# Agent attention and gated convolution: loads held to a fixed time ahead of use, and other rows in the shifted copies

## The chip, the cores and the metric

The kernel runs on one core of a Trainium2 chip. The core has TensorE (PE, matrix products into PSUM), VectorE (DVE), ScalarE (ACT), GpSimd (POOL) and SyncE (SP, which here issues nearly all DMAs). The time of a run is in microseconds on the device; several runs are made and the median is told. The profile is one further look at a single execution: its span goes from the first to the last instruction of the program.

## What is computed

Two stages. First agent attention: 49 agents gather from 12800 keys, and 12800 queries gather from the agents. Then a gated unit with a causal convolution of 5 taps.

```python
def sm(a, b):                       # softmax over the last axis
    s = scale * (a @ b.transpose(0, 2, 1))
    s = s - s.max(-1, keepdims=True)
    e = np.exp(s)
    return e / (e.sum(-1, keepdims=True) + 1e-09)
a2k = sm(agents, k)                 # (4, 49, 12800)
agent_v = a2k @ v                   # (4, 49, 128)
q2a = sm(q, agents)                 # (4, 12800, 49)
x = q2a @ agent_v                   # (4, 12800, 128)
...
for k in range(K):                  # K = 5, xp is x with 4 rows of zeros ahead
    gate_pre += conv_w[k][None, None, :] * xp[:, k:k + S, :]
gate = 1.0 / (1.0 + np.exp(-gate_pre))
val = x @ w_val
out = gate * val @ w_out
```

q, k, v have shape (4, 12800, 128), agents (4, 49, 128).

## The kernel before

The x of the reference is never formed. The attention weights q2a (49 numbers a row) are themselves the input of the gated stage, and agent_v is folded into the weights of that stage once a batch: `fold_weights` makes, for each of the 5 taps and for w_val, a matrix that takes 128 rows of attention weights to 128 channels.

**Units and chunks.** A batch of 12800 rows is cut into 10 units of 1280 rows for the attention and into 25 chunks of 512 rows for the gated stage. Two units, that is five chunks, make a segment of 2560 rows. There are 4 batches, 40 units, 20 segments and 100 chunks (the last one in two halves).

**Steps.** Each unit has a key step k (`key_scores`: 16 score matmuls at L376, a copy on ScalarE, a maximum on DVE), a value step v (`agent_values`: exponentials, a block transpose on DVE, 40 matmuls at L480), a query step q (`queries`) and a transpose step t (`transposes`). Each chunk has a gate step g (`gates`: five matmuls at L922, one at L926, a tanh at L935), a value step a (`values`: L949, L953, the product h at L962, its upper half hh at L968 on ScalarE, its lower half hl at L973 on GpSimd) and an output step o (`project`: L992 to L994, a scaled copy at L1006, the store). "max" and "fold" are the key maximum and the folding of weights, once a batch.

**Precision by pairs.** Products of the gated stage are made in fp16 from sums of an upper and a lower half. A weight of 49 agents is thus 49 numbers upper and 49 lower, and products upper x upper, lower x upper and upper x lower are wanted: 147 rows for a matrix that has 128. So `queries` builds the tile pt with 128 columns a row: 49 lower halves (L794, GpSimd), 49 upper halves (L779, ScalarE), and 30 of the upper halves a second time (L784, GpSimd), to be met with the lower halves of the folded weights. The 19 agents that don't fit go into a second stationary: for these, x2 holds 19 x 5 = 95 rows, each agent's upper half at the five shifts of the convolution, and L926 and L953 multiply them. Which agents are doubled in pt and which 19 go to x2 is a choice; the folded weights in `wst` (tile rows 2A and up, and the rows TAPS+1 and TAPS+2) must follow the same choice. Before, of the first 45 agents two in three are doubled in pt and every third goes to x2 with the last four.

**Transposes and shifts.** pt must be turned, so that its 128 columns lie on partitions. For the first four units PE does that; for the others a DMA transpose from pt into the tile x1 (L835). Then `shifts` copies the 19 rows of x1, five times each at shifts of one element, into x2 by two DMAs (L884), one for each entry of X2CUTS: 15 source partitions with step 3, then 4 with step 1. From the third segment on this is done once for a segment, behind the transpose of its second unit. `halo` copies the last 4 columns of a segment to the head of the next, on GpSimd (L819).

**Loads.** `load` brings a unit of k, q or v into one of NLOAD = 11 slots of the tile ld, in the order of use (L369). A load may start when the last use of its slot is done.

**The plan.** Nothing is issued at once. Each step is put into a `Plan` with its engine, a cost in us, and what it reads and writes. PE's steps keep their order, which is written out by hand in a long string. `Plan.order` then plays the steps through: it keeps a time for each engine, lets the engine that can start first do so, takes among the open steps the one with the longest tail of work behind it, and models the DMA by one wire with a cost for each transfer (1.57 for a load, 2.4 for a transpose, the numbers in X2CUTS for x2). A step is open from the time `at` that its inputs are ready. The steps are emitted sorted by their start in this play. Each engine's queue, SP's too, then runs in that order on the chip; the times of the play are not kept, only the order. A load has no input but its free slot, so in the play it is open as soon as the slot is.

Of the kernel before, what the change touches and what calls it, by code (L numbers as in the profile page):

```python
# [13 lines left out]
ALU = mybir.AluOpType  # L14
# [13 lines left out]
TAPS = 5  # L28
HALO = TAPS - 1
PAD = 16  # L30


THREES = 15
NDUP = 2 * THREES
X2R = 19
X2CUTS = ((0, THREES, 3, 0.5), (THREES, X2R, 1, 0.3))


NLOAD = 11
# [1 line left out]
NPT = 4  # L41
# [17 lines left out]
BACKLOG = 3.0  # L59
LANES = 8  # L60
LAND = 1.4

QS = 256.0
WS = 64.0
# [3 lines left out]
class Plan:  # L68
# [11 lines left out]
    def add(self, engine, us, fn, reads=(), writes=(), moved=0.0, key=None, urge=0.0):  # L80
        i = len(self.steps)
        need = set()
        for x in reads:
            need |= self.wrote.get(x, set())
        for x in writes:
            need |= self.wrote.get(x, set()) | self.read.get(x, set())
        for x in reads:
            self.read.setdefault(x, set()).add(i)
        for x in writes:
            self.wrote[x], self.read[x] = {i}, set()  # L90
        self.steps.append((engine, us, fn, need, moved, key))
        self.urge.append(urge)

    def order(self):
        n = len(self.steps)
        after = [[] for _ in range(n)]
        last = None
# [16 lines left out]
        wire = 0.0  # L114
        lanes = [0.0] * LANES
        left = [len(s[3]) for s in self.steps]
        at = [0.0] * n
        queues = {e: [] for e in engines}
        pe = [i for i, s in enumerate(self.steps) if s[0] == "pe"]
        here = 0  # L120
# [50 lines left out]
                        queues[self.steps[j][0]].append(j)  # L171
        self.start = start
        return sorted(range(n), key=lambda i: (start[i], i))


@with_exitstack
def tile_agent_attention_gated_conv(
# [9 lines left out]
    nc = tc.nc  # L187
# [166 lines left out]
    def load(kind, b, u):  # L354
        i = taken[0] % NLOAD
        taken[0] += 1
        slot_of[kind, b, u] = i
        if kind == "v":
            dst, src = ld[i], vP[b, u].rearrange("p n c -> p (n c)")
        else:  # L360
            dst = ld[i][:, 0:UNIT]
            src = (kT if kind == "k" else qT)[b, :, u * UNIT : (u + 1) * UNIT]
        parts = [(dst, src, [("ld", i), ("ld2", i)])]
        if (kind, b, u) == ("v", 0, NU - 1):
            h = VW // 2
            parts = [(dst[:, 0:h], src[:, 0:h], [("ld", i)]), (dst[:, h:], src[:, h:], [("ld2", i)])]
        for d, f, keys in parts:
            add(
                "dma", 0.4, lambda d=d, f=f: nc.sync.dma_start(out=d, in_=f), (), keys,  # L369
                1.57 / len(parts),  # L370
            )

    def score_matmuls(b, src, out):
# [139 lines left out]
    def fold_weights(b):  # L513
# [58 lines left out]
        ghi = wst[:, 0:TAPS, 0:A]  # L572
        vhi = wst[:, TAPS, 0:A]

        def threes(x):

            if len(x.shape) == 2:
                return x[:, 0 : 3 * THREES].rearrange("p (i r) -> p i r", r=3)
            return x[:, :, 0 : 3 * THREES].rearrange("p k (i r) -> p k i r", r=3)

        def rest(out, full, s, hi):
            dve.scalar_tensor_tensor(
                out=out, in0=full, scalar=rs[:, s : s + 1], in1=hi,
                op0=ALU.mult, op1=ALU.subtract,
            )

        def val_weights():
            dve.tensor_reduce(
                out=mx[:, 1:2], in_=pv[:, 0:A], axis=AX.X, op=ALU.max,
                apply_absolute_value=True,  # L590
            )
            dve.tensor_scalar(
                out=mx[:, 1:2], in0=mx[:, 1:2], scalar1=TINY, scalar2=1.0 / WS,
                op0=ALU.max, op1=ALU.mult,
            )
            dve.reciprocal(out=rs[:, 1:2], in_=mx[:, 1:2])
            dve.tensor_scalar_mul(vhi, pv[:, 0:A], rs[:, 1:2])
            pv3, hi3 = threes(pv[:, 0:A]), threes(vhi)
            rest(
                wst[:, TAPS, 2 * A :].rearrange("p (i r) -> p i r", r=2),  # L600
                pv3[:, :, 0:2], 1, hi3[:, :, 0:2],
            )
            rest(x2v[:, HALO, 0:THREES], pv3[:, :, 2], 1, hi3[:, :, 2])
            rest(x2v[:, HALO, THREES:], pv[:, 3 * THREES : A], 1, vhi[:, 3 * THREES :])

        def gate_weights():
            dve.tensor_scalar_mul(ghi, gw, rs[:, 0:1])
# [6 lines left out]
        def gate_rest_pool():  # L614
            def less(out, full, hi):
                nc.gpsimd.tensor_tensor(out=out, in0=full, in1=hi, op=ALU.subtract)

            gs3, hi3 = threes(gs), threes(ghi)
            twos = wst[:, 0:TAPS, 2 * A :].rearrange("p k (i r) -> p k i r", r=2)
            for r in range(2):  # L620
                less(twos[:, :, :, r], gs3[:, :, :, r], hi3[:, :, :, r])
            less(x2g[:, :, 0:THREES], gs3[:, :, :, 2], hi3[:, :, :, 2])
            less(x2g[:, :, THREES:], gs[:, :, 3 * THREES :], ghi[:, :, 3 * THREES :])

        def gate_rest():
            gw3, hi3 = threes(gw), threes(ghi)
            twos = wst[:, 0:TAPS, 2 * A :].rearrange("p k (i r) -> p k i r", r=2)
            for r in range(2):
                rest(twos[:, :, :, r], gw3[:, :, :, r], 0, hi3[:, :, :, r])
            rest(x2g[:, :, 0:THREES], gw3[:, :, :, 2], 0, hi3[:, :, :, 2])  # L630
            rest(x2g[:, :, THREES:], gw[:, :, 3 * THREES :], 0, ghi[:, :, 3 * THREES :])

        w_ = ("wst", x)

# [98 lines left out]
    def queries(b, u):  # L733
# [28 lines left out]
        def sums():  # L762
# [16 lines left out]
            "act", 0.58, lambda: nc.scalar.copy(out=pt[:, :, A : 2 * A], in_=w),  # L779
            [("qw", g % NPT)], [(*p_, 0)],  # L780
        )
        add(
            "pool", 0.44,
            lambda: nc.gpsimd.tensor_scalar(  # L784
                out=pt[:, :, 2 * A :].rearrange("p n (i r) -> p n i r", r=2),
                in0=w[:, :, 0 : 3 * THREES].rearrange("p n (i r) -> p n i r", r=3)[:, :, :, 0:2],
                scalar1=1.0, scalar2=0.0,
                op0=ALU.mult, op1=ALU.add,
            ),
            [("qw", g % NPT)], [(*p_, 2)],  # L790
        )
        add(
            "pool", 1.09,
            lambda: nc.gpsimd.tensor_tensor(  # L794
# [71 lines left out]
    def shifts(b, u):  # L866

        g = b * NU + u
        if g >= SINGLE and g % 2 == 0:
            return  # L870
        n = 1 if g < SINGLE else 2
        u0 = u + 1 - n
        s = g // 2
        x2, x1 = x2s[s % 3], x1s[s % NX]
        o = (g + 1 - n) % 2 * UNIT
        src = row_keys(s, range(0, g % 2 + 1))
        c = PAD - HALO + o
        for r0, r1, every, us in X2CUTS:
            first = A + (2 if every == 3 else 3 * THREES)
            rows = x1[first : first + 1 + (r1 - r0 - 1) * every : every, c : c + 1]  # L880
            view = [rows.ap[0], (1, TAPS), (1, n * UNIT)]
            add(
                "dma", 0.6,
                lambda r0=r0, r1=r1, rows=rows, view=view: nc.sync.dma_start(  # L884
                    out=x2[r0 * TAPS : r1 * TAPS, o : o + n * UNIT],
                    in_=bass.AP(rows.tensor, rows.offset, view),
                ),
                src, [("x2", s % 3, o + i * UNIT, r0) for i in range(n)], us * n,
            )
        if g % 2 and (g + 1) // 2 < B * NU // 2:  # L890
            halo((g + 1) // 2)
# [246 lines left out]
            done += 1  # L1138
        run[w[0]](*w[1:])

    for i in plan.order():
        plan.steps[i][2]()


# [42 lines left out]
```

## Time and profile before

| | |
|---|---|
| median of 3 runs | 428.5 us (428.43 to 429.73) |
| span of the profiled execution | 423.6 us |
| that execution's own time | not listed |
| mean granted TensorE clock | 0.985 |
| read from and written to HBM | 79.25 MB, 26.21 MB |

Busy times of the engines are shares of the span; they say who is full, not who sets the end. What an engine waits for is listed by pairs: the engine and line that waited, what ended the wait, the sum in us, the number of times, and the longest. For SP the list gives the times its queue stood. A window row gives, for a stretch of time, the busy time of each engine, then the clock that was granted to TensorE as a share of full speed, the mean busy share of the 16 DMA engines (over 1 where packets overlap) and the rate in GB/s. A row of the timeline has the start, the duration, engine, line, operation and tiles; for SP the duration is that of the issue, not of the transfer.

### The profile page before, as it was taken

What the parts mean: (1) busy time and instruction counts of PE and PEld (TensorE: products, weight loads), DVE (VectorE), ACT (ScalarE), POOL (GpSimd) and SP (SyncE); (2) the same over time, 40 slices, a digit from 0 to 9 for tenths busy, and PEclk for the clock granted to TensorE, in tenths of its full rate; (3) what the DMA queues carried; (4) which work ended last, traced back from release to release, by engine and by line L of the source; (5) the groups of instructions that cost most, each with busy time, mean ns of one, the idle gap of its engine ahead of it and who ended that gap; (6) DMA issues with size and microseconds to landing.
All of it is one profiled execution on the core that took longest, in us unless ns stands there. A gap on an engine that the chain in (4) does not pass through costs nothing.

```text
span 423.6 us, 10042 instructions
## 1 busy us (share of the span) xinstructions
PE 403.9 (95%) x3907; PEld 197.0 (47%) x3907; DVE 293.3 (69%) x562; ACT 301.5 (71%) x521; POOL 228.2 (54%) x263
## 2 busy tenths in 40 slices
PE   4979999999999999999999899999999989999995
PEld 1358434346555443446555343335555534344443
DVE  3757899867875978667795575767765678676231
ACT  1564568779966777678876486778876567788776
POOL 1002557654657565554566355574366277877553
PEclk9969999999999999999999899999999999999998
DMA  8999999999999999999999999999999977755733
GB/s 320 420 417 411 370 367 353 301 295 310 412 293 283 346 317 362 304 278 356 351 379 324 271 299 370 314 332 302 296 393 322 239 196 161 199 163 176 205 121 124
DMA packets 75129, 127.62 MB, mean 301 GB/s; under 512 B 50466, under 2 KB 50850, under 8 KB 75084
## 3 DMA queue, kind: packets, MB, share of 16 engines
q1 hardware_dynamic: 74940, 126.87, 96.9%
q8 instruction: 30, 0.49, 0.5%
q10 hardware_dynamic: 144, 0.13, 0.2%
q14 instruction: 15, 0.12, 0.1%
HBM read 79.25 MB, written 26.21 MB: 249 GB/s over the span
## 4 chain that ended last, share of the span: by engine, by line
PE 78%; DMA 9%; DVE 8%; ACT 1%; POOL 1%; issue 1%; SPq 0%; POOLq 0%; DVEq 0%; ACTq 0%
PE gate L922 23%; PE sc L376 17%; PE av L480 10%; PE val L949 5%; PE out L992 5%; PE val L953 5%; PE gate L926 5%; PE out L993 4%; DMA ld<-kT 4%; PE out L994 4%; DMA x<-pt 3%; DMA x<-x 2%; DVE h L962 1%; DVE qw L772 1%; DVE qsm L763 1%
## 5 line engine op out<-in xcount | busy, mean ns | idle before, releaser
L973 POOL TENSOR_TENSOR hl<-h,hh 128x512 f16<-128x512 f32 (+1 forms) x101 | 116.9, 1158 | 96.1 <-ACT hh L968 96.0
L922 PE MATMUL gate<-x,stat 128*128 128x512 f16 (+1 forms) x500 | 125.2, 380 | 0.2 <-ACT th L935 0.2
L962 DVE SCALAR_TENSOR_TENSOR h<-th,val 128x512 f32<-128x512 f32 x100 | 67.8, 678 | 66.8 <-PE out L993 26.2
L376 PE MATMUL sc<-ld,ag_sb 128*32 128x320 f32 x1280 | 101.5, 447 | 7.6 <-DMA ld<-kT 7.0
L935 ACT ACTIVATE th<-gate,unscale 128x512 f32<-128x512 f32 x100 | 68.3, 683 | 33.3 <-PE gate L926 31.7
L1006 ACT ACTIVATE ob<-out,oscale 128x512 f32<-128x512 f32 x98 | 67.3, 687 | 21.3 <-PE out L994 20.1
L922 PEld LDWEIGHTS <-stat 128*128 128x128 f16 x505 | 46.3, 97 | 63.7 <-issue 14.8
L968 ACT CAST hh<-h 128x512 f16<-128x512 f32 (+1 forms) x101 | 61.5, 609 | 17.2 <-DVE h L962 16.4
L750 POOL TENSOR_TENSOR qw<-sT,qmx 128x490 f32<-128x490 f32 x40 | 41.4, 1035 | 47.6 <-DVE qmx L745 47.5
L376 PEld LDWEIGHTS sc<-ld,ag_sb 128*32 128x32 f32 x1280 | 36.7, 111 | 59.4 <-issue 25.7
L480 PE MATMUL av<-ld,eT 128*32 128x129 f32 (+1 forms) x1400 | 50.7, 279 | 1.0 <-DVE eT L386 1.0
L480 PEld LDWEIGHTS av<-ld,eT 128*32 128x32 f32 (+1 forms) x1400 | 47.1, 117 | 7.5 <-issue 2.5
L794 POOL TENSOR_TENSOR pt<-qw,pt 128x490 f16<-128x490 f32 x40 | 44.8, 1120 | 3.1 <-ACT pt L779 2.9
L471 ACT ACTIVATE e<-ks,kbias 128x320 f32<-128x320 f32 x80 | 39.3, 554 | 5.4 <-DVE eT L386 3.3
L386 DVE STREAM_TRANSPOSE sT<-sc 128x640 f32<-128x640 f32 x40 | 33.6, 839 | 13.4 <-PE sc L376 12.7
L402 ACT COPY ks<-sc 128x640 f32<-128x640 f32 x40 | 27.7, 691 | 21.2 <-PE sc L376 19.1
L386 DVE STREAM_TRANSPOSE eT<-e 128x640 f32<-128x640 f32 x40 | 33.5, 842 | 9.8 <-ACT e L471 5.2
L926 PE MATMUL gate<-x,stat 95*128 95x512 f16 x100 | 38.3, 383 | 1.5 <-DMA x<-x 1.5
L949 PE MATMUL val<-x,stat 128*128 128x512 f16 x100 | 38.2, 382 | 0.8 <-DVE h L962 0.6
L953 PE MATMUL val<-x,stat 95*128 95x512 f16 x100 | 38.1, 381 | 0.0
L994 PE MATMUL out<-hl,wo 128*128 128x512 f16 x98 | 37.0, 378 | 1.1 <-POOL hl L973 1.1
L992 PE MATMUL out<-hh,wo 128*128 128x512 f16 x98 | 37.3, 381 | 0.1
(130 smaller groups left out, 389.4 us busy)
## 6 DMA issues: line engine op xcount, KB each, us to landing
ld<-kT SPq DMA_DIRECT2D x40, 640.0 KB
ld<-qT SPq DMA_DIRECT2D x40, 640.0 KB
ld<-vP SPq DMA_DIRECT2D x39, 645.0 KB
outT<-ob SPq DMA_DIRECT2D x48, 512.0 KB
x<-x SPq DMA_DIRECT2D x18, 375.0 KB
x<-x SPq DMA_DIRECT2D x18, 100.0 KB
outT<-ob SPq DMA_DIRECT2D x3, 256.0 KB
x<-x SPq DMA_DIRECT2D x4, 187.5 KB
```

The costliest lines, as they stand in the source:

```text
L376: nc.tensor.matmul(out=out[g * BLK : (g + 1) * BLK, j, 0:GT], lhsT=ag_sb[:, b, j * BLK : (j + 1) * BLK], rhs=src[:, g * GT : (g + 1) * GT] ...
L386: nc.vector.transpose(out=out.rearrange("p n (j i) -> p j n i", j=2), in_=in_.rearrange("p j (n i) -> p j n i", i=BLK),)
L480: nc.tensor.matmul(out=av[o + j : o + j + cols, 0 : C + 1], lhsT=et[:, n, j : j + cols], rhs=vt[:, n, :], start=(u == 0 and n < 2), stop=( ...
L922: nc.tensor.matmul(out=pg, lhsT=stat[:, k, :], rhs=x1[:, c : c + w], start=(k == 0), stop=False,)
L926: nc.tensor.matmul(out=pg, lhsT=stat[0 : TAPS * X2R, TAPS + 1, :], rhs=x2[0 : TAPS * X2R, o2 : o2 + w], start=False, stop=True,)
L935: lambda: nc.scalar.activation(out=th, in_=pg, func=AF.Tanh, scale=unscale[:, 0:1]),
L949: nc.tensor.matmul(out=pv, lhsT=stat[:, TAPS, :], rhs=x1s[(b * NCH + n0 // CH) // 5 % NX][:, PAD + o2 : PAD + o2 + w], start=True, stop=False,
L953: nc.tensor.matmul(out=pv, lhsT=stat[0 : TAPS * X2R, TAPS + 2, :], rhs=x2[0 : TAPS * X2R, o2 : o2 + w], start=False, stop=True,)
L962: lambda: nc.vector.scalar_tensor_tensor(out=h, in0=th, scalar=1.0, in1=pv, op0=ALU.add, op1=ALU.mult),
L968: "act", 0.16 + 0.42 * scale, lambda: nc.scalar.copy(out=hh, in_=h),
L973: lambda: nc.gpsimd.tensor_tensor(out=hl, in0=h, in1=hh, op=ALU.subtract),
L1006: lambda: nc.scalar.activation(out=ob[:, o : o + w], in_=po, func=AF.Copy, scale=oscale),
```

## The change

Three things.

**The hold.** Loads get a key "ld". The plan is played once as before. Then, for every load, the start of its first user in that play less AHEAD = 20 us is taken as the earliest time at which the load is open, and the plan is played again with these times. The steps are emitted in the order of the second play. The program gets no timer and no new wait by it: a load's place in SP's queue moves.

**Other rows in x2.** The doubled upper halves in pt are now those of the 24 odd agents and of six agents 2, 10, ... 42; x2 takes the 13 agents 0, 4, ... 48 and the six 6, 14, ... 46. So the two DMAs into x2 read 13 source partitions with step 4 and 6 with step 8, 19 as before. The costs given to the plan change from 0.5 and 0.3 to 0.45 and 0.25 us a unit.

**What follows from the rows.** The copy of doubled halves in `queries` becomes two GpSimd instructions of 240 and 60 elements (cost 0.64 for 0.44 in the plan). In `fold_weights` the lower halves of the weights are written in four pieces: for the gate these were four before, for the value three.

```diff
-THREES = 15
-NDUP = 2 * THREES
+ODD = 24
+NDUP = 30
 X2R = 19
-X2CUTS = ((0, THREES, 3, 0.5), (THREES, X2R, 1, 0.3))
+FOURS = 13
+X2CUTS = ((0, FOURS, 0, 4, 0.45), (FOURS, X2R, 6, 8, 0.25))
...
+AHEAD = 20.0
...
-    def order(self):
+    def order(self, held=None):
...
-        at = [0.0] * n
+        at = list(held or [0.0] * n)
...
+    def late_loads(self):
+        self.order()
+        held = [0.0] * len(self.steps)
+        for i, s in enumerate(self.steps):
+            for j in s[3]:
+                if self.steps[j][5] == "ld":
+                    t = self.start[i] - AHEAD
+                    held[j] = min(held[j], t) if held[j] else t
+        return self.order(held)
...
-                1.57 / len(parts),
+                1.57 / len(parts), key="ld",
...
+        def pick(x, first, every):
+            return x[:, first:A:every] if len(x.shape) == 2 else x[:, :, first:A:every]
+
+        def lows(low, full, hi, less):
+            for out, first, every, n in (
+                (low[0], 1, 2, ODD), (low[1], 2, 8, NDUP - ODD), (low[2], 0, 4, FOURS), (low[3], 6, 8, X2R - FOURS),
+            ):
+                less(out, pick(full, first, every), pick(hi, first, every))
...
-        add(
-            "pool", 0.44,
-            lambda: nc.gpsimd.tensor_scalar(
-                out=pt[:, :, 2 * A :].rearrange("p n (i r) -> p n i r", r=2),
-                in0=w[:, :, 0 : 3 * THREES].rearrange("p n (i r) -> p n i r", r=3)[:, :, :, 0:2],
-                scalar1=1.0, scalar2=0.0,
-                op0=ALU.mult, op1=ALU.add,
-            ),
-            [("qw", g % NPT)], [(*p_, 2)],
-        )
+
+        def again():
+            for o, n, first, every in ((2 * A, ODD, 1, 2), (2 * A + ODD, NDUP - ODD, 2, 8)):
+                nc.gpsimd.tensor_scalar(
+                    out=pt[:, :, o : o + n], in0=w[:, :, first : A - 1 : every],
+                    scalar1=1.0, scalar2=0.0, op0=ALU.mult, op1=ALU.add,
+                )
+
+        add("pool", 0.64, again, [("qw", g % NPT)], [(*p_, 2)])
...
-        for r0, r1, every, us in X2CUTS:
-            first = A + (2 if every == 3 else 3 * THREES)
+        for r0, r1, first, every, us in X2CUTS:
+            first += A
...
-    for i in plan.order():
+    for i in plan.late_loads():
         plan.steps[i][2]()
```

The writing of the weights' lower halves by `lows` (value weights by DVE; the gate's by GpSimd for the first batch, by DVE for the others) takes the place of the same instructions on slices of three.

More of the change, by code (lines that the diff above doesn't have):

```diff
@@ L573, in fold_weights @@
         vhi = wst[:, TAPS, 0:A]
[L575 to L579, printed above, removed]
+        def pick(x, first, every):
[5 more added lines that the diff above has]
+                less(out, pick(full, first, every), pick(hi, first, every))
         def rest(out, full, s, hi):
@@ L597, in val_weights @@
             dve.tensor_scalar_mul(vhi, pv[:, 0:A], rs[:, 1:2])
[L598 to L601, printed above, removed]
-            )
-            rest(x2v[:, HALO, 0:THREES], pv3[:, :, 2], 1, hi3[:, :, 2])
-            rest(x2v[:, HALO, THREES:], pv[:, 3 * THREES : A], 1, vhi[:, 3 * THREES :])
+            low = (
+                wst[:, TAPS, 2 * A : 2 * A + ODD], wst[:, TAPS, 2 * A + ODD :],
+                x2v[:, HALO, 0:FOURS], x2v[:, HALO, FOURS:],
+            )
+            lows(low, pv[:, 0:A], vhi, lambda out, full, hi: rest(out, full, 1, hi))
+        gate_lows = (
+            wst[:, 0:TAPS, 2 * A : 2 * A + ODD], wst[:, 0:TAPS, 2 * A + ODD :],
+            x2g[:, :, 0:FOURS], x2g[:, :, FOURS:],
+        )
         def gate_weights():
@@ L616, in less @@
                 nc.gpsimd.tensor_tensor(out=out, in0=full, in1=hi, op=ALU.subtract)
[L618 to L623, printed above, removed]
-        def gate_rest():
[L626 to L631, printed above, removed]
+            lows(gate_lows, gs, ghi, less)
+        def gate_rest():
+            lows(gate_lows, gw, ghi, lambda out, full, hi: rest(out, full, 0, hi))
         w_ = ("wst", x)
@@ L781, in queries @@
         )
-        add(
-            "pool", 0.44,
-            lambda: nc.gpsimd.tensor_scalar(
-                out=pt[:, :, 2 * A :].rearrange("p n (i r) -> p n i r", r=2),
-                in0=w[:, :, 0 : 3 * THREES].rearrange("p n (i r) -> p n i r", r=3)[:, :, :, 0:2],
-                scalar1=1.0, scalar2=0.0,
-                op0=ALU.mult, op1=ALU.add,
-            ),
-            [("qw", g % NPT)], [(*p_, 2)],
-        )
+        def again():
[3 more added lines that the diff above has]
+                    scalar1=1.0, scalar2=0.0, op0=ALU.mult, op1=ALU.add,
+                )
+        add("pool", 0.64, again, [("qw", g % NPT)], [(*p_, 2)])
         add(
```

## The prediction

> **What bounds the kernel now.** I read the page first: the span, the busy shares, the granted clock, the DMA rows.
>
> ```profile
> span 423.6 us, 10042 instructions
> PE 403.9 (95%) x3907; PEld 197.0 (47%) x3907; DVE 293.3 (69%) x562; ACT 301.5 (71%) x521; POOL 228.2 (54%) x263
> ...
> DMA  8999999999999999999999999999999977755733
> ...
> q1 hardware_dynamic: 74940, 126.87, 96.9%
> ```
>
> Two resources stand near their limit: TensorE, and the 16 DMA engines, which have packets under way nearly all the time up to slice 32 (about 340 us) and only then get air. To tell which of them sets the end, I asked what PE waits for between 60 us, when the steady work has begun, and 415 us, when it is over. This is the whole answer:
>
> ```profile
> PE gate L926 <- DMA x<-x: 1.5, 1, 1.5
> PE out L994 <- POOL hl L973: 1.1, 1, 1.1
> PE val L949 <- DVE h L962: 0.6, 1, 0.6
> PE gate L922 <- ACT th L935: 0.2, 1, 0.2
> ```
>
> In 355 us PE waits four times, 3.4 us together. The other 351 us are matmuls, back to back in the order written out by hand, which the change leaves as it is. So PE is the bound, and a busy DMA costs time only where it makes one of these waits. The first wait shows in the windows of 10 us, where PE has less than 10.00 (the columns: stretch, length, busy time and count of PE, PEld, DVE, ACT, POOL, granted clock, DMA share and GB/s):
>
> ```profile
> 10.00:20.00 10.00, 9.32 (x120) 3.72 (x111) 7.54 (x15) 4.88 (x8) 0.00 (x0) 1.00 1.02 419
> ...
> 230.00:240.00 10.00, 8.50 (x107) 4.72 (x100) 5.10 (x14) 3.67 (x7) 4.97 (x7) 0.85 1.14 290
> 240.00:250.00 10.00, 10.00 (x84) 4.63 (x83) 7.23 (x21) 7.23 (x14) 5.70 (x8) 0.98 1.11 270
> ```
>
> The first wait has a second price: behind it the granted clock falls to 0.85 over one window and 0.98 over the next, which is 10 x 0.15 + 10 x 0.02 = 1.7 us of full-speed work lost. It costs 1.5 + 1.7 = 3.2 us. The second and the third cost 1.1 and 0.6. **All that can be won in steady state is 3.2 + 1.1 + 0.6 + 0.2 = 5.1 us.**
>
> The chain of waits tells where the first two come from (start, length, what):
>
> ```profile
> 220.73 7.50 DMA x<-pt
> ...
> 228.28 7.34 DMA x<-x
> ...
> 331.87 6.86 DMA x<-pt
> ...
> 338.78 0.19 POOL x L819
> 338.97 2.23 POOL hl L973 x2
> ```
>
> At the first place it is a DMA transpose (7.50 us from issue to landing) and then the shifted copies into x2 (7.34 us) that gate's last matmul waits for. At the second, near 338 us, it is a transpose of 6.86 us; the halo copy on GpSimd (L819) waits for it with two hl subtractions behind it in GpSimd's order, and PE waits for hl. Both places end in a DMA that is slow because others are queued before it.
>
> **The held loads.** SP's own order of issue, early, around the first place, around the second, and late; then the chain's rows of the score matmuls (sc, 16 for a unit of 1280 rows) that use these loads:
>
> ```profile
> 45.45 1.04 SPq L369 DMA_DIRECT2D ld<-kT  x2
> ...
> 208.55 0.33 SPq L369 DMA_DIRECT2D ld<-qT  x1
> 208.97 0.45 SPq L369 DMA_DIRECT2D ld<-kT  x1
> ...
> 211.21 0.33 SPq L369 DMA_DIRECT2D ld<-kT  x1
> 212.77 7.23 SPq L835 DMA_TRANSPOSE x<-pt  x1
> 220.10 0.53 SPq L369 DMA_DIRECT2D ld<-kT  x1
> ...
> 326.31 2.14 SPq L369 DMA_DIRECT2D ld<-qT  x2
> ...
> 385.03 1.37 SPq L835 DMA_TRANSPOSE x<-pt  x1
> ```
>
> ```profile
> 56.44 2.36 PE sc L376 x32
> ...
> 241.27 2.29 PE sc L376 x32
> ...
> 247.80 1.21 PE sc L376 x16
> ...
> 252.70 2.29 PE sc L376 x32
> ...
> 368.32 1.21 PE sc L376 x16
> ...
> 379.83 1.21 PE sc L376 x16
> ```
>
> Counting the loads of each kind along the written order, the issues at 208.55 and 208.97 are q2.4 and k3.0, used in the 32 matmuls at 241.27: a lead of 32 us. The next two, k3.1 at 211.21 and k3.2 at 220.10, are used at 247.80 and 252.70. With the hold at 20 us these four would be issued at about 221, 222, 228 and 233 us, behind the two transposes instead of before them. A load is 640 KB at the 419 GB/s of the window from 10 to 20 us, so 1.56 us of all engines: 3 x 1.56 = 4.7 us leave the stretch before the first transpose, and a fourth load, 0.53 us of SP's own time at 220.10, leaves the place before the second. SP needs 7.23 us to issue the transpose at 212.77, and 1.37 us for the same instruction at 385.03, where the DMA row shows a 3: that is the backlog, and the hold takes most of it out. The second transpose is free to go when GpSimd has done its pt:
>
> ```profile
> 219.51 0.45 POOL L784 TENSOR_SCALAR pt<-qw 128x300 f16<-128x300 f32 x1
> ...
> POOL x L819 <- DMA x<-pt: 16.4, 5, 6.0
> ```
>
> It is ready at 219.96, went out at 220.73, and should land up to 0.8 + 4.7 = 5.5 us earlier, and x2 with it; the wait of 1.5 us needs 1.5 of that. I take the wait and its 1.7 us of clock as gone: **-3.2 us**.
>
> At the second place the two loads issued at 326.31 are q3.8 and q3.9, used at 368.32 and 379.83; held, they go out near 348 and 360. Another 2 x 1.56 = 3.1 us ahead of the transpose at 331.87 go. GpSimd's 6.0 us before L819 (the longest wait in the last row) shrink by up to that, more than the 1.1 us that PE waited for hl: **-1.1 us**. The 0.6 us, PE waiting for an h of DVE, I leave.
>
> What the hold moves later must find room. The four last q loads pass 340 us, 4 x 1.56 = 6 us of DMA into a stretch in which the DMA row shows 3 to 7: they are hidden. Before 60 us the loads run closer than 20 us ahead of use (the two at 45.45, k1.3 and k1.4, are used by 56.44), so there the hold binds nothing: 0. No instruction gets a new wait. What changes is who stands behind whom on SP: a held load now stands behind transposes that wait for GpSimd, and PE is behind the load.
>
> **The rows of x2.** The same 95 rows of 5 KB in two DMAs: 15 + 4 source partitions with 5 taps before, 13 + 6 after. The list of DMA issues has their sizes, and that of a load:
>
> ```profile
> ld<-kT SPq DMA_DIRECT2D x40, 640.0 KB
> ...
> x<-x SPq DMA_DIRECT2D x18, 375.0 KB
> x<-x SPq DMA_DIRECT2D x18, 100.0 KB
> ```
>
> Bytes are equal (475 KB a pair); how they spread over the engines no row shows. Bounds: no change, or at best the surplus of 7.34 us over the 1.56 x 475/640 = 1.2 us that the bytes need at full rate; a worse spread could add a like amount. I take 0, because PE waits for x<-x once in this stretch and that wait is already counted as gone. [...]
>
> **GpSimd's second instruction and the folds.** The copy of doubled rows becomes two instructions, 240 and 60 elements, for one of 300.
>
> ```profile
> L784 POOL TENSOR_SCALAR pt<-qw x40: 439/448/799, 39.7 to 389.1; 128x300 f16<-128x300 f32 x40
> ```
>
> 300 elements take 0.448 us, and the copy of 4 elements at L819 took 0.19: 0.9 ns an element, so 0.39 + 0.24 = 0.63 us from below; two such instructions at the old price, 0.90, from above. I take 0.70, that is +0.25 us a unit and 10 us in 40 units, 228 to 238 us of GpSimd. In steady state the cover is the room between a unit's pt and its chunks: each transpose goes out 0.25 us later, which the earlier landing above outweighs. Without that cover it is 0.25 us each time PE waits for x2, once. Uncovered are the first four units, whose pt goes through PE; between 40 and 60 us PE waits for it once:
>
> ```profile
> PE sc L849 <- POOL pt L794: 0.2, 1, 0.2
> ```
>
> That wait grows: +0.25. val_weights has four rest instructions in place of three; the chain has seven of this line in 1.48 us, 0.21 us each:
>
> ```profile
> 343.10 1.48 DVE wst L582 x7
> ```
>
> In the first fold this stands before PE's first chunk, +0.2; in the three later folds chunks of the batch before cover it. Sum **+0.4 us**.
>
> **The sum** is -3.2 - 1.1 + 0.4 = -3.9 us against the profiled span, 423.6 to 419.7. The time of the profiled execution itself is not given; the median of the runs, 428.5, lies 4.9 us above its span, and I take these 4.9 us as unchanged: **424.6 us**.
>
> **Rivals.** First, **the same time**, because the transpose is late for another reason, or the hold is an order of the plan that the chip does not keep.
>
> ```profile
> SPq L835 <- POOL hl L973: 48.4, 17, 8.1
> ...
> SPq L835 <- POOL pt L784: 19.2, 6, 7.2
> ```
>
> SP waits 48.4 and 19.2 us for GpSimd before transposes: where pt is late, fewer loads ahead don't help. For it speaks that pt of the second transpose was ready only just before 220; against it the 7.23 us of issue, which is no wait for pt. Then -3.2 shrinks to nothing, or moves to another segment: 428 to 429. The new costs and the second run of the plan also sort DVE, ScalarE and GpSimd anew; each new meeting costs what the old ones did, 0.6 to 1.1 us, and three of them give the gain back. That the hold does nothing (leads of the plan already short) gives 428.5 + 0.4 = 428.9; the 32 us above speak against it.
>
> Second, **slower**, by a load that comes late. A held load stands behind a transpose in SP's order; SP can stand for 8.1 us on GpSimd and for 7.23 us in the issue, and a DMA issued into a backlog lands 7.3 to 7.5 us on. 20 - 8.1 - 7.2 - 7.5 = -2.8: in the worst meeting of rows PE waits 2.8 us and loses a further 1.7 by the clock, 4.5 us. It decides from the point where SP holds a load more than 20 - 7.5 = 12.5 us behind its place. One such event gives 424.6 + 4.5 = 429.1, two give 433.6. Against it: the backlog that makes both long is what the hold takes away, and before 60 us shorter leads do without such a wait.
>
> Third, **both places and the 0.6 go, and x2 is quicker too**: 428.5 - 5.1 = 423.4 and, with as much as 1 us of small waits before 60 us trimmed, 422.4.
>
> **Chances.** My forecast with the third case (422.4 to 427.2): 0.62; below that 0.03; the same time, both versions (427.2 to 429.8): 0.20; slower through late loads (429.8 to 434): 0.15. What a measurement can tell from no change is 0.3%, 1.3 us. Faster 0.65, same 0.20, slower 0.15. The range 422.3 to 429.9 leaves out 0.03 below and 0.15 above.
>
> **What would show it.** The held loads: SP's order has three fewer loads just before the transposes of 212 us, these are issued in less than 4 us, the DMA row has slices under 9 ahead of slice 32, and the last loads are issued near 360 us. The first place: no PE wait for x<-x and a clock of 1.00 between 230 and 250. The second: L819's wait under 4 us and no PE wait for hl. GpSimd: two groups in place of L784 with 0.6 to 0.8 us together. Wrong would be a row in which PE waits for ld<-qT, ld<-kT or ld<-vP after 60 us, a new clock dip, or a wait for x<-x at another segment.

## The result, and the profile after

The changed kernel takes 420.47 us (median of 7 runs, 419.6 to 427.83), the kernel before on the same chip 427.43 us (7 runs, 425.47 to 429.73). The ratio is 0.9849 with a 95% interval of 0.9815 to 0.9884; the run of 427.83 us, at a mean clock of 0.986, is a slow one and is left out of it. Some 6.5 us are gained where 3.9 were forecast, and the time lies below the lower end of the range, 422.3 us.

The profiled execution of the kernel after took 423.02 us, with a span of 420.0 us; the five other runs that the ratio uses have spans of 417.5 to 418.4 us, so what follows is read from a longer execution than most. The page's rows that answer to those of before:

```profile
span 420.0 us, 10094 instructions
...
PE 399.0 (95%) x3907; PEld 193.0 (46%) x3907; DVE 295.0 (70%) x566; ACT 301.0 (72%) x521; POOL 237.0 (56%) x303
...
DMA  8999999999999999999999999999999999996633
...
q1 hardware_dynamic: 74940, 126.87, 99.4%
```

The number of matmuls is the same (3907), and GpSimd is busy 237 us as forecast (238). But the DMA engines are not less loaded before slice 32, as the prediction expected: the row of nines runs on to slice 36. The same bytes have been spread over a longer stretch, and the share of the queue went up from 96.9% to 99.4%. What PE waits for between 60 and 412 us, the whole answer:

```profile
PE gate L937 <- DMA x<-x: 1.9, 2, 1.1
PE gate L933 <- ACT th L946: 0.2, 1, 0.2
```

The waits for hl (1.1 us) and for h (0.6 us) are gone. A wait for the shifted copies in x2 is still there, and there are two of them. The first is at the old place; the windows of the kernel after (columns as before):

```profile
230.00:240.00 10.00, 8.91 (x124) 5.28 (x116) 6.20 (x18) 4.89 (x8) 4.95 (x6) 1.00 1.12 317
240.00:250.00 10.00, 10.00 (x78) 4.42 (x70) 8.13 (x24) 7.93 (x14) 6.68 (x9) 1.00 1.09 305
```

PE idles 10.00 - 8.91 = 1.1 us instead of 1.5, and this time no dip of the clock follows. The second is at a segment where before had none; the timeline of PE shows it, and ahead of it a group of score matmuls that will serve as a clock for the loads:

```profile
238.79 2.36 PE L390 MATMUL sc<-ld,ag_sb 128*32 128x320 f32 x32
...
331.62 0.39 PE L937 MATMUL gate<-x,stat 95*128 95x512 f16 x1 [0.83 <-DMA x<-x]
```

SP's own order around the first place, and at the end, in the kernel after:

```profile
209.21 0.33 SPq L383 DMA_DIRECT2D ld<-qT  x1
...
211.94 6.09 SPq L846 DMA_TRANSPOSE x<-pt  x1
218.14 1.15 SPq L383 DMA_DIRECT2D ld<-vP  x1
219.39 3.28 SPq L846 DMA_TRANSPOSE x<-pt  x1
...
224.30 0.38 SPq L383 DMA_DIRECT2D ld<-qT  x1
...
227.60 1.70 SPq L895 DMA_DIRECT2D x<-x  x2
...
357.56 1.44 SPq L383 DMA_DIRECT2D ld<-qT  x1
```

The load that was issued at 208.55 before (q2.4) now goes out at 224.30, for the matmuls at 238.79: a lead of 14.5 us in place of 32. The hold does what it says, and more, since the plan meant 20 us. Other loads, with earlier uses, have moved into the place in front of the transpose: in the 12 us ahead of it SP issues seven loads in both kernels, and the issue still takes 6.09 us. The second transpose follows at 219.39 instead of 220.73. The chain of waits shows both landings:

```profile
219.39 8.13 DMA x<-pt
...
228.54 6.35 DMA x<-x
```

From issue to landing nothing is clearly quicker. The transpose takes 8.13 us where before had 7.50. The 6.35 us begin at the second of the two copies into x2, where the 7.34 of before began at the first; from the first issue, at 227.60, to the same end it is 7.29 us. What moved is the moment of issue.

### The profile page after: what moved, and what is told of

Its sections match the earlier page's. It is cut to its first block, busy times and chain, and to the rows that moved or that the text cites. A ratio compares the mean times of both kernels' runs of the same rounds, so it can differ in the third digit from the quotient of the medians.

```text
span 420.0 us, 10094 instructions
## 1 busy us (share of the span) xinstructions
PE 399.0 (95%) x3907; PEld 193.0 (46%) x3907; DVE 295.0 (70%) x566; ACT 301.0 (72%) x521; POOL 237.0 (56%) x303
## 3 DMA queue, kind: packets, MB, share of 16 engines
q1 hardware_dynamic: 74940, 126.87, 99.4%
## 4 chain that ended last, share of the span: by engine, by line
PE 75%; DMA 18%; DVE 3%; ACT 1%; SPq 1%; issue 1%; POOLq 0%; POOL 0%; DVEq 0%
PE gate L933 22%; PE sc L390 17%; DMA ld<-vP 6%; PE av L494 6%; DMA x<-pt 5%; PE val L960 5%; PE gate L937 5%; PE out L1003 5%; PE val L964 5%; DMA x<-x 5%; PE out L1004 4%; PE out L1005 4%; DMA ld<-kT 2%; DVE qw L784 0%; SPq L895 0%
## 5 line engine op out<-in xcount | busy, mean ns | idle before, releaser
L494 PE MATMUL av<-ld,eT 128*32 128x129 f32 (+1 forms) x1400 | 48.9, 273 | 2.5 <-DMA ld<-vP 1.4
L494 PEld LDWEIGHTS av<-ld,eT 128*32 128x32 f32 (+1 forms) x1400 | 44.2, 113 | 10.0 <-issue 3.3
L797 POOL TENSOR_SCALAR pt<-qw 128x240 f16<-128x240 f32 x80 | 27.4, 362 | 22.6 <-DVE qw L784 22.6
```

Of the source, the lines that this page charges most:

```text
L494: nc.tensor.matmul(out=av[o + j : o + j + cols, 0 : C + 1], lhsT=et[:, n, j : j + cols], rhs=vt[:, n, :], start=(u == 0 and n < 2), stop=( ...
```

## The experiments

Three theories stood at the start. The first: the hold alone makes the gain, by letting SP come to its transposes sooner; the rows of x2 and the second GpSimd instruction do nothing that can be measured. The second: the other rows of x2 make the gain, by shorter copies. The third: the gain is mostly TensorE's clock, since the profiled execution of before has a mean granted clock of 0.985 and that of after 0.999, and 0.014 x 424 = 6 us is the size of the whole gain.

Kernels of one group ran on one chip and share the runs of the kernel before: median 426.67 us in the first group (23 runs), 426.26 in the second (23), 426.63 in the third (17). Here are all twelve; the last column is PE's waits between 60 and 412 us in one profiled execution, without the 0.2 us for th that nearly every kernel has.

| kernel | ratio and 95% interval | median us | PE waits |
|---|---|---|---|
| copy of before | 0.9984 [0.9958, 1.0010] | 426.54 | 3.5 |
| copy of after | 0.9868 [0.9828, 0.9908] | 421.37 | 2.4 |
| before + hold | 0.9842 [0.9810, 0.9874] | 420.01 | 0 |
| after without the hold | 0.9970 [0.9935, 1.0005] | 426.59 | 3.8 |
| hold + two GpSimd copies | 0.9886 [0.9844, 0.9927] | 420.76 | 0.6 |
| hold + the new plan costs | 0.9879 [0.9842, 0.9917] | 420.27 | 0 |
| hold for uses before 150 us | 1.0030 [1.0003, 1.0057] | 427.43 | 4.8 |
| hold for uses from 150 us on | 1.0052 [1.0023, 1.0081] | 428.12 | 7.2 |
| hold of 30 us | 0.9968 [0.9941, 0.9994] | 425.67 | 2.1 |
| hold of 12 us | 1.0137 [1.0088, 1.0186] | 432.67 | 10.4 |
| hold from 40 down to 20 us | 0.9893 [0.9857, 0.9929] | 421.72 | 0.3 |
| another copy of before (one run) | | 427.85 | 5.6 |

### Before and after once more

Both kernels unchanged, to see how much one execution differs from the next.

> The kernel before, again, for the spread of its spans and clocks. Three theories. HOLD: the held loads make the gain. ROWS: the other rows of x2 make it, by shorter copies. CLOCK: the gain is mostly the granted clock, which dipped twice in the first profile of before (mean 0.985) and not in that of after (0.999). All expect a ratio of 1.00 here. HOLD and ROWS expect a mean clock like that of after in most of its runs (0.995 and over) and spans near 422 to 424 all the same; CLOCK expects most of its runs near 0.985 and spans that come within 1.5 us of those of after once the lost clock is taken off.

> The changed kernel, again, on the same chip. All expect a ratio of 0.983 to 0.988, as first measured. CLOCK expects mean clocks of 0.995 and over and no stretch below 1.00 between 20 and 40 us or behind the wait near 234 us; HOLD and ROWS expect about the clocks of before.

Before against itself is 0.9984 [0.9958, 1.0010]. After is 0.9868, so the gain in this group is 426.67 - 421.37 = 5.3 us. The median clock of before, 0.992, lies between the 0.985 and the 0.995 that the theories named. Of PE's waits in this second execution of before, these three are the longest:

```profile
PE out L994 <- POOL hl L973: 1.3, 1, 1.3
PE gate L926 <- DMA x<-x: 1.1, 2, 0.7
PE val L949 <- DVE h L962: 0.6, 1, 0.6
```

The hl and h waits stand where they stood, but the wait for x<-x of 1.5 us at 234 us is now two short ones: 0.4 us at the old place, and 0.7 us near 94 us, where the execution that the prediction was read from had no such wait. There is no clock dip in the middle of this execution, its span is 422.1 us, and its time 424.11. So the dip, and the size of the wait, 3.2 us together on which the prediction built most of its gain, belong to one execution of before, not to the kernel.

A third execution of before was profiled in the last group.

> A third look at the kernel before. Its first profile had no PE wait near 94 us and its second one of 0.7 us, and a kernel with the same order up to there had 2.7 us. If the waits at the tight segments change from execution to execution, this one shows another set of them, at x<-x and hl, of 1 to 6 us together; if they are fixed, 1.1 to 1.5 for x<-x near 234 us, 1.1 to 1.3 for hl and 0.6 for h.

This time the span is 425.8 us, and the waits are

```profile
PE gate L926 <- DMA x<-x: 2.5, 2, 2.3
PE av L432 <- DVE m L425: 1.3, 1, 1.3
PE out L994 <- POOL hl L973: 1.2, 1, 1.2
PE val L949 <- DVE h L962: 0.6, 1, 0.6
```

with the longest at 235 us, the old place, again (0.2 of the 2.5 us are near 95 us):

```profile
230.00:240.00 10.00, 7.69 (x118) 4.73 (x118) 5.26 (x11) 3.84 (x7) 3.87 (x5) 1.00 1.14 335
```

Neither recorded reading holds for all of them: the waits for hl and h are much the same each time, the ones for x2 and m change. Three executions of one kernel give 3.4, 3.7 and 5.8 us of PE's waits with the 0.2 us for th, and spans of 423.6, 422.1 and 425.8 us. The median of the 23 spans in the first group is 424.6 us: the execution in the prediction was one of the better ones.

### The hold alone

```diff
+AHEAD = 20.0
-    def order(self):
+    def order(self, held=None):
-        at = [0.0] * n
+        at = list(held or [0.0] * n)
+    def late_loads(self):
...
-    for i in plan.order():
+    for i in plan.late_loads():
```

This is before with the second planning run and the key "ld", and nothing of the rows, of GpSimd's copies or of the plan's costs.

> The kernel before with the hold alone (two runs of the plan, 20 us), its own rows in x2 and its own GpSimd copy. HOLD: 0.984 to 0.990, that is 4 to 7 us. ROWS: 0.998 to 1.003. CLOCK: as much of the gain as it raises the mean clock, 0.1% of time for 0.001 of clock.

It gives 0.9842 [0.9810, 0.9874], 420.01 us: all of the gain. On its page:

```profile
span 417.7 us, 10047 instructions
...
DMA  8999999999999999999999999999999999989723
```

Between 60 and 412 us PE waits for nothing but this:

```profile
PE gate L933 <- ACT th L946: 0.2, 1, 0.2
```

The DMA engines are as full as in the kernel after (the queue's share is 99.5% against 99.4%), and PE waits for no DMA between 60 and 412 us. SP's order around the first place:

```profile
210.87 5.09 SPq L846 DMA_TRANSPOSE x<-pt  x1
216.06 1.21 SPq L380 DMA_DIRECT2D ld<-vP  x1
217.38 3.24 SPq L846 DMA_TRANSPOSE x<-pt  x1
```

The first transpose takes SP 5.09 us instead of 7.23, and the second goes out at 217.38 instead of 220.73, 3.3 us sooner. The window of that place now is

```profile
230.00:240.00 10.00, 9.99 (x134) 5.71 (x123) 7.28 (x23) 5.43 (x11) 6.19 (x7) 1.00 1.19 281
```

Against the clock theory: the median of the mean granted clock over the 23 runs of before is 0.992, over the 6 runs of this kernel 0.994, and 0.002 x 424 is under 1 us of 6.7. The 0.985 of the first execution of before was low, and the 0.999 of after was high. The two kernels of the second group that also have the whole hold (below) have median clocks of 0.991 and 0.992, no more than before, and gain over 1% all the same.

**What else the second play moves.** The edit lets the second play order every engine anew, not SP alone. Put side by side, the traces of before and of the hold alone have the same order on PE, DVE and ScalarE. On SP, besides loads, two stores change place. On GpSimd eight instructions do: six halo copies or hl subtractions between 70 and 263 us, a qw at 299 us, and one at a place where PE waited. GpSimd's timeline in before:

```profile
338.78 0.19 POOL L819 COPY x<-x 128x4 f16<-128x4 f16 x1 [5.99 <-DMA x<-pt]
338.93 2.27 POOL L973 TENSOR_TENSOR hl<-h,hh 128x512 f16<-128x512 f32 x2
```

and with the hold alone:

```profile
329.89 1.17 POOL L984 TENSOR_TENSOR hl<-h,hh 128x512 f16<-128x512 f32 x1 [0.86 <-ACT hh L979]
333.94 0.19 POOL L830 COPY x<-x 128x4 f16<-128x4 f16 x1 [2.88 <-DMA x<-pt]
334.09 1.16 POOL L984 TENSOR_TENSOR hl<-h,hh 128x512 f16<-128x512 f32 x1
```

The hl that PE waited for in before now stands ahead of the halo copy, done at 331.06 for a matmul at 335.10. In the old order it would have run behind the copy, at 334.09 to 335.25: PE's wait would have been some 0.2 us instead of 1.1. So two things took this wait away: the transpose landed earlier, by about 1 us as PE counts, which alone is nearly enough by these rows, and GpSimd's order changed, which alone is enough. The h that PE waited 0.6 us for comes on DVE behind the fold's work, which in before waits 2.1 us for a product of GpSimd (L541); that stood behind both hl, at 341.15 us, and now stands behind one, at 335.20. No run has the loads held and GpSimd's old order, so what the moves on GpSimd bring by themselves is not measured; in the waits at this place it is at most 1.1 + 0.6 us. At 234 us GpSimd's order is that of before, and the hold of 30 us, which has the same swap at 338 us, gains little (below).

### The rows alone

```diff
-    for i in plan.late_loads():
+    for i in plan.order():
```

This is after without its hold.

> The changed kernel with its first plan, without the hold: other rows in x2, two GpSimd copies, the new costs. HOLD: 0.999 to 1.003, the GpSimd copy costing up to 0.4 us. ROWS: 0.984 to 0.990. CLOCK: as for the hold alone, by its mean clock.

It gives 0.9970 [0.9935, 1.0005], no difference that can be told. The waits of before are all there:

```profile
PE gate L937 <- DMA x<-x: 1.7, 1, 1.7
PE out L1005 <- POOL hl L984: 1.5, 1, 1.5
PE val L960 <- DVE h L973: 0.6, 1, 0.6
```

The ratio lies a little under the range that the first theory named (0.999 to 1.003). Only the place of the x<-x wait has changed, from 234 us to 137 us:

```profile
130.00:140.00 10.00, 8.30 (x118) 4.87 (x117) 7.01 (x18) 4.78 (x9) 5.78 (x8) 0.93 1.12 311
140.00:150.00 10.00, 10.00 (x93) 4.47 (x92) 7.19 (x22) 5.83 (x11) 4.09 (x7) 0.90 0.98 296
```

Here the clock does dip behind the wait, 0.93 and then 0.90. The second theory falls, and of the first stands that the hold alone makes the gain.

### The second GpSimd instruction, and the plan's costs

To the hold alone one piece each was added. First the copy in two instructions of 150 elements, at the plan's old cost:

```diff
+        def again():
+            for r in range(2):
+                nc.gpsimd.tensor_scalar(
+                    out=pt[:, :, 2 * A + r :: 2], in0=w[:, :, r : 3 * THREES : 3],
+                    scalar1=1.0, scalar2=0.0, op0=ALU.mult, op1=ALU.add,
+                )
+        add("pool", 0.44, again, [("qw", g % NPT)], [(*p_, 2)])
```

> The hold alone, and the GpSimd copy of the doubled halves in two instructions of 150 elements with the old rows and the old cost in the plan. The hold alone gave 0.984 and the whole change 0.987. If the second GpSimd instruction is what the rest of the change gives back: 0.986 to 0.990, with a PE wait for x<-x near 234 or 331 us again. If it is the new costs or the new rows: 0.983 to 0.986 and no PE wait over 0.5 us after 60 us.

The group of this copy, on the page's form (busy time of one at its shortest, its median and its longest, in ns):

```profile
L795 POOL TENSOR_SCALAR pt<-qw x80: 390/404/763, 39.2 to 384.8; 128x150 f16<-128x150 f32 x80
```

The pair takes 2 x 0.404 = 0.81 us where one instruction took 0.448, more than the pair in after (below), and the kernel is at 0.9886 [0.9844, 0.9927], 420.76 us. Then the plan's new prices on the old instructions:

```diff
-            "pool", 0.44,
+            "pool", 0.64,
-X2CUTS = ((0, THREES, 3, 0.5), (THREES, X2R, 1, 0.3))
+X2CUTS = ((0, THREES, 3, 0.45), (THREES, X2R, 1, 0.25))
```

> The hold alone, with the new costs in the plan (0.64 for the GpSimd copy, 0.45 and 0.25 for x2) and the old instructions. If the costs sort the queues worse: 0.986 to 0.990 with a PE wait for x<-x. If it is the second instruction or the rows: 0.983 to 0.986.

0.9879 [0.9842, 0.9917], 420.27 us, and no wait for x<-x. Both kernels have the ratio of the one recorded reading (0.986 to 0.990) and the waits of the other (0.3 us and none for x<-x). Both ratios lie just above the interval of the hold alone, [0.9810, 0.9874], and their own intervals overlap with it. So neither piece brings anything, and what it costs, if anything, is too small for these runs to tell.

### Half of the hold

```diff
-                if self.steps[j][5] == "ld":
+                if self.steps[j][5] == "ld" and self.start[i] < 150.0:
```

and in a second kernel the same with `>= 150.0`: only the loads whose use the plan puts before, or after, 150 us are held. The question was which of the places gives the gain.

> The hold for loads whose first user starts before 150 us in the plan, none for the others. My prediction put all of the gain at two places after 200 us: then this gives 0.997 to 1.001. If the hold also frees the segments whose x2 lands within 1.5 us of its use near 94 and 136 us in before, which cost time in other executions than the profiled ones: 0.990 to 0.996, 2 to 4 us.

> The hold for loads whose first user starts at 150 us or later in the plan. By my prediction 0.984 to 0.989, all of the gain. If the early segments have a share of it: 0.989 to 0.994, and the gains of the two halves add up to that of the whole.

Each half is a little slower than before, 1.0030 and 1.0052, outside of every range that was recorded, although both together are 0.984. In the first PE waits 4.8 us for x<-x, once. SP's order ahead of it:

```profile
210.28 0.33 SPq L380 DMA_DIRECT2D ld<-qT  x1
...
215.37 0.33 SPq L380 DMA_DIRECT2D ld<-kT  x1
216.85 7.28 SPq L846 DMA_TRANSPOSE x<-pt  x1
224.85 2.65 SPq L846 DMA_TRANSPOSE x<-pt  x1
...
228.71 2.68 SPq L846 DMA_TRANSPOSE x<-pt  x1
```

Past the edge the loads that are no longer held go out ahead of the transposes, as they did in before; the second transpose leaves at 224.85, 4.1 us later than in before, and PE waits 4.8 us at 234 us. A part of that, at most 2.8 us, has another cause: in this order the next segment's transpose, at 228.71, stands ahead of the copies into x2, which go out behind it at 231.49; in before the copies go first (228.28) and that transpose follows (230.04). The second half has its long wait at the other side of the edge:

```profile
PE sc L387 <- DMA ld<-kT: 4.5, 1, 4.5
PE gate L937 <- DMA x<-x: 2.7, 1, 2.7
```

The first row is a held load that came too late, at 142.9 us, where the early loads end and the held ones begin:

```profile
147.45 2.36 PE L387 MATMUL sc<-ld,ag_sb 128*32 128x320 f32 x16 [4.51 <-DMA ld<-kT]
```

The second row is one wait that ends at 96.7 us. There SP's order is still that of before, whose three executions waited 0, 0.7 and 0.2 us at this place; so these 2.7 us are no price of the edge.

The halves thus measure their own edges and not the share of a place. What they do show is the size of both prices: loads and a transpose ahead of what PE needs, 4.8 us, and a load held too long behind what stands before it, 4.5 us. The waits for hl and h near 338 us are gone in both halves. In the late half the loads there are held, and the hl stands ahead of the halo copy. In the early half neither is so; but there PE has lost 4.8 us at 234 us, while SP issues the copies behind that transpose at 339.62 against 338.78 in before, 0.84 us later: PE comes to the place after its data. A wait is a difference between two engines, and a longer one earlier covers it.

### The length of the hold

The hold alone, with AHEAD = 30.0 and AHEAD = 12.0, and with a hold that has no edge:

```diff
-                    t = self.start[i] - AHEAD
+                    t = self.start[i] - AHEAD * (1.0 + min(1.0, max(0.0, (200.0 - self.start[i]) / 80.0)))
```

which is 40 us for uses before 120 us, falling to 20 us at 200 us.

> The hold alone with 30 us in place of 20. The question is whether the gain comes from a fixed lead as such or from how short it is. If short leads leave the DMA free for the transposes: a part of the gain, 0.988 to 0.997, with waits for x<-x or hl left over. If any hold will do, because the second run of the plan sorts the rest better: 0.982 to 0.987. If the hold stops biting at 30 us: 0.998 to 1.002.

> The hold alone with 12 us. With 20 us the loads went out 12 to 15 us ahead of use on the chip after 160 us, and they need 8 to 9 us to land. My rival of the late load expects PE waits for ld<-qT, ld<-kT and ld<-vP, several of 1 to 4 us, and 1.01 to 1.06. If the shorter lead also shortens the backlog by as much: 0.982 to 0.990.

> The hold alone with 40 us for first users before 120 us in the plan, falling evenly to 20 us at 200 us: the late half without the edge at 150 us at which a key load came 4.5 us late. If the late half failed for its edge alone, and the places near 234 and 338 us make most of the gain: 0.988 to 0.992. If the early half is needed too, for the waits near 94 and 136 us: 0.993 to 0.999.

A hold of 30 us gives 0.9968, a third of a per cent from nothing and over a full per cent from that of 20 us. A wait of 0.8 us for x2 near 94 us is left, beside one of 1.3 us for m, as in the third execution of before. That profile is of the fastest of the kernel's 12 runs, 423.19 us, and does not show what the others lose.

A hold of 12 us is slower, 1.0137. There PE waits for the loads themselves:

```profile
PE av L491 <- DMA ld<-vP: 5.1, 5, 1.9
PE sc L387 <- DMA ld<-qT: 2.6, 3, 1.3
PE sc L387 <- DMA ld<-kT: 2.4, 2, 2.2
```

10.1 us in ten waits, against 432.67 - 420.01 = 12.7 us to the hold of 20. So the gain sits in a narrow valley. From issue to landing the loads of the hold alone took 7.1 us (k), 6.4 (q) and 7.0 (v), medians over the whole program, where the recorded text has 8 to 9. On the chip the lead that the plan means to be 20 us came out at 13.6 us (median of the q and k loads used after 160 us in the hold alone; 10 to 20), that of 30 us at 21.9 (17 to 28), and that of 12 us at 9.2 (5 to 16). Why the chip's lead is shorter is not settled; that SP comes late to its DMAs while it stands in an issue was only argued.

The hold without an edge gives 0.9893, 421.72 us: 426.63 - 421.72 = 4.9 of the 6.7 us that the hold alone brings, with the loads used before 120 us left much as they were. Its only wait for x2 is 0.3 us, near 94 us.

So most of the gain is at the late places (234 us, 331 to 338 us), and up to some 2 us at the early ones (94 and 137 us); the intervals overlap, so the second number is a direction and not a size.

## Why the prediction was wrong

The sign was right, and so was the kind of the mechanism, that the place of the loads in SP's queue sets PE's waits. The time was 424.6 - 420.5 = 4.1 us too high. Two steps failed.

**"The median of the runs shown, 428.5, lies 4.9 us above its span, and I take these 4.9 us as unchanged."** The median time of the runs of after lies 420.5 - 418.4 = 2.1 us above their median span, so this step carries 2.8 of the 4.1 us; the span, 419.7 against 418.4, carries the rest. In the runs of all kernels the time lies 1.9 to 2.3 us above the span of the same execution (medians; 2.0 in the 23 runs of before). The 4.9 us were three things: some 2.0 us of this kind; 1.0 us by which the profiled span of 423.6 was better than the typical 424.6; and 1.8 us by which the three runs shown, 428.5, were above the 426.7 of 23 runs. With 419.7 + 2.0 the same sum would have given 421.7 us, 1.2 us from the result, but that would have been partly luck: counted from the typical span it gives 424.6 - 3.9 + 2.0 = 422.7 us, and the 2.2 us left are a gain that was put too small.

**"All that can be won in steady state is 3.2 + 1.1 + 0.6 + 0.2 = 5.1 us."** The ceiling was read from one execution, and 4.3 of it were counted as won. The other two executions of before have other waits at other places: the mean of PE's waits is (3.4 + 3.7 + 5.8) / 3 = 4.3 us, of which the hold leaves 0.2. The mean of the three spans, 423.8 us, stands 6.1 us above the 417.7 of the hold alone, and PE's timeline tells where they lie. The first score matmuls after 60 us (q0.5) start at 60.69, 60.03 and 61.51 us in before and at 60.25 with the hold, the last ones (q3.9) at 379.76, 378.30 and 381.94 against 374.05. So 0.5 us are won before 60 us, 5.5 between these two, and 0.2 behind. Of the 5.5, 4.1 are the waits; the other 1.4 us are 2.1 in the execution with the dip of the clock and 1.0 in the other two, and where that 1.0 comes from is open. In place of 4.3 us won in steady state and 0.4 lost outside, the hold alone won 5.5 and some 0.7.

The terms, one by one:

- **The first place, -3.2.** Right in kind for the hold alone, where no x<-x wait is left and the clock is 1.00. In the kernel after 1.1 of the 1.5 us are left in its profiled execution, and a new wait of 0.83 us stands at 331 us. The 1.7 us of clock were chance: behind the 2.3 us in the third execution of before no dip follows. The 4.7 us of loads did not leave the stretch before the first transpose, because the loads ahead of them move back too and take their places: seven loads go out in the 12 us ahead of it before and after, six in the hold alone. The second transpose goes out 1.3 us earlier in after and 3.3 in the hold alone, not up to 5.5.
- **The working of that place.** The prediction took GpSimd's pt for the second transpose to be ready at 219.96. That row belongs to a later unit. The timeline of GpSimd in before has its own copies here:

```profile
212.77 1.09 POOL L794 TENSOR_TENSOR pt<-qw,pt 128x490 f16<-128x490 f32 x1
213.83 0.45 POOL L784 TENSOR_SCALAR pt<-qw 128x300 f16<-128x300 f32 x1
```

  pt was done at 213.83 + 0.45 = 214.28, and the transpose left 6.4 us later: SP was in the issue of the first transpose (7.23 us) and of one load. That issue is therefore the price itself, not only a sign of backlog. The 1.37 us that it was compared with, at 385.03, belong to slice 36 of the DMA row, which shows a 5; the 3 that the prediction names are slices 38 and 39. For the same reason the rival of the same time, "the transpose is late for another reason", had no ground here.
- **The second place, -1.1.** The number came, the working only in part. PE's wait for hl is gone, and the halo copy waits 2.99 us in place of 6.0, below the 4 us that were named. But in after, too, an hl now runs between pt and the halo copy, and it fills 2.0 of the 3.0 us. From the end of the pt instruction ahead to the copy it is 338.78 - 332.79 = 5.99 us in before and 335.40 - 330.40 = 5.0 in after: by GpSimd's count the transpose lands 1.0 us sooner, not up to 3.1. The prediction left the order on GpSimd as it was.
- **The 0.6 us of h, left.** Wrong: it goes with the hl wait, in every kernel whose hold reaches that place, and stays in before and in the rows alone, where nothing is held.
- **The GpSimd copy, 0.70 us a unit, and the folds, +0.4.** The size is right, the price is not seen. The groups of the two (the last number ahead of the second bar is the mean of one, in ns):

```profile
L797 POOL TENSOR_SCALAR pt<-qw 128x240 f16<-128x240 f32 x40 | 17.1, 427 | 22.6 <-DVE qw L784 22.6
L797 POOL TENSOR_SCALAR pt<-qw 128x60 f16<-128x60 f32 x40 | 11.8, 296 | 0.0
```

  A pair takes 0.427 + 0.296 = 0.72 us, where 0.70 was forecast. The hold with an even dearer pair (0.81 us) has an interval that overlaps with that of the hold alone. Nor is there a loss before 60 us: the score matmuls of q0.5 start at 60.40 us in after, against 60.03 to 61.51 in before.
- **The rows of x2, 0.** Right as far as can be told: rows without the hold give 0.9970 [0.9935, 1.0005], the hold without the rows 0.9842 and with them 0.9868, with intervals that overlap. That after has waits of 1.9 and 2.4 us for x<-x in two executions, and the kernels with the hold and the old rows 0 to 0.3, may speak against the rows by a microsecond. But both profiles are of longer executions, with spans of 420.0 and 420.6 us, where 8 of the 12 spans behind the two ratios of after are at most 418.4; it is not settled. At the first place the pair of copies landed 7.29 us after its first issue in after and 7.34 us in before: no earlier landing shows there, and no view shows how the copies spread over the DMA engines.
- **The slower rival, by late loads.** It did not come at 20 us: PE waits for no load after 60 us. It came where the hold was made 8 us shorter (10.1 us of waits for loads), and once at the edge of the late half, where the wait alone was 4.5 us and not the 2.8 that were named. The margin was real, and less than 8 us.
- **What would show it.** The shorter leads, the two GpSimd groups, the clock of 1.00, the halo copy and the missing wait for hl came as named, and the last load goes out at 357.56. Four signs did not come: PE still waits for x<-x at the first place, there are not three fewer loads ahead of the transpose, its issue takes 6.09 us and not under 4, and the DMA row has no slice under 9 ahead of slice 32. One sign of being wrong came, a wait for x<-x at another segment (331 us). The hold takes no bytes away; other transfers move up.

## What to carry to other kernels

In this kernel the DMA queue is full nearly all the time (a share of 96.9% before, 99.5% with the hold alone), and the order in it sets PE's waits: in before a load issued at 208.55, 32 us ahead of its use, stood in front of a transpose issued at 220.73, and PE started on the x2 behind that transpose at 235.67, 15 us later, after a wait of 1.5 us. Holding the loads back brought 1.6% without a byte less, in a narrow valley between too early and too late (0.9968 with 30 us, 0.9842 with 20, 1.0137 with 12). Before a gain is put down to one queue, see what else the same edit has moved on the other engines. Before a sum is made against one profiled execution, place its span among the spans of several, and take the time as span plus the overhead of the same execution. Here a hold that began or ended in the middle of the program made a burst or a gap at its edge (PE waits of 4.8 and 4.5 us), so the experiment by halves measured the edge.

## What the hardware showed that was not expected

- The issue of one transpose held SP for 1.37 us where the DMA row shows a 5 (before, 385.03) and for 7.23 us where it shows a 9 (212.77). SP's next issue came only after it, at 386.73 and at 220.10.
- In these runs a drop of the granted clock behind a PE wait did not go by the wait's length: 1.5 us (before, first execution; down to 0.85) and 1.7 us (rows alone; 0.90) had one, 2.3 us (before, third execution), 2.7 us (late half, near 94 us) and 1.1 us (after) had none, with 1.00 in the windows around them; the two longest, 4.8 and 4.5 us in the halves, had one (0.87 and 0.83).
- GpSimd's time for this copy grew slowly with its elements: in the mean 0.296 us for 60 and 0.427 for 240 (after) and 0.457 for 300 (before). In the median one of 150 took 0.404 us and one of 300 0.448, so two of 150, 0.81 us, cost nearly twice one of 300. (The strides differ too.)
